# Fused attention and two expert layers: the last two of five value products moved one step later

## The chip, the cores and the metric

The kernel runs on one NeuronCore of a Trainium2 chip. The metric is device time in microseconds (us). The engines are named as in the profile: PE (TensorE, matmuls and transposes), PEld (its weight loads), DVE (VectorE), ACT (ScalarE), POOL (GpSimd), SP (SyncE, which issues the DMAs).

## The reference

Three layers in a row, in float32:

- Attention for 4 batches of 8 heads, sequence 576, head size 64: `scores = q @ k.T / 8 + decay`, causally masked, softmax over the keys, times `v`. The decay comes from a running sum of log forget gates.
- A soft mixture of experts over the 2304 tokens of width 512: `logits = x @ phi` for 32 slots, a softmax over the *tokens* (dispatch) that makes 32 slot inputs, 8 small experts, and a softmax over the slots (combine).
- A second mixture: 4 dense experts 512 to 1024 to 512, weighted by given probabilities.

## The kernel before, in words

**Pairs and steps.** Attention works on pairs of heads, `pr` from 0 to 15, four pairs to a batch. A pair has seven steps (`NS`), `g = 7 * pr + st`. A step computes the scores of one head's block of queries: step 0 the first two blocks of 128 queries of the even head, step 1 the fourth, step 2 the third, step 3 the last 64 queries of both heads together (`j == 4`), steps 4 to 6 the odd head's blocks in the order of steps 0 to 2. The main loop (L490) does, for every `g`: `scores(g)`, then `before_tr(g)`, then `transposes(g - 2)`, then `after_tr(g)`. So the transposes in step `st` belong to the scores of two steps before, and what `before_tr` and `after_tr` do belongs to the pair before.

**One step's chain.** `scores` runs two products of reduced-precision parts on PE into one of four PSUM tiles (L227, L228; L212 for step 3). DVE adds the mask and takes the maximum (L198, in two pieces for step 3), ACT computes the exponential with its row sums (L202). Two steps later PE transposes the probabilities (L249 for the first two blocks, L253 for the others, L260 for the last 64 columns) into one of two PSUM tiles; DVE or ACT copies them to SBUF, to `pta` (two blocks) or `ptb` (the other three).

**Values.** `av_a` (L289, step 1 of the next pair) multiplies the first two blocks by `v`; `av_b` (L277, step 2) does the other three blocks, 320 query columns, as five products over the five blocks of keys: 320 columns for the first three, 192 for the fourth, 64 columns of 64 keys for the fifth, each for two heads, each as two PE instructions. They add up in one PSUM tile. After the fifth ACT copies the sum into `ot` (L280) and SP loads `v` of the next pair into the one buffer there is for it (L133). `av_a` of the next pair is its first reader.

**After the values.** `nat` transposes `ot` back and DVE scales it by the row sums into `xn`, the rows of `x` (L304, L310). `logits` multiplies `ot` by `phi` (L325), and for a batch's last pair `rep4` lays the logits out for transposes. In the first pair of the next batch the finished batch's dispatch softmax runs: `dlog` transposes the logits (step 2, L372) and has DVE and ACT take maximum and exponential (L376, L381), `csoft1` and `csoft2` do the combine softmax, `dnat` transposes the exponentials back (step 4, L396, copied at L398), and `sadd` adds the tokens' share to the 32 slot sums (L407, L413). `xn` has one buffer, so the sums of a batch must have read it before `nat` of the next batch's first pair writes it.

**What sets the order.** In attention PE's instructions run in the order of the code (`tc.manual_schedule(engines={E.PE})`). For DVE, ACT, POOL and SP a planner of the framework orders the instructions by its own cost model and by when their inputs come; each engine then runs its list in order. The PSUM tiles of values, sums, `nat` and logits come in turn from one pool of two buffers (tag "av"), those of the transposes from another of two (tag "pt"), from which `dlog` takes one too. The splitting of the next pair's `q` and `k` into two parts each (`split_a`, `split_b`: ACT, DVE, POOL) is written between `scores` and `before_tr`, at steps 3, 4, 6 and 0, with the loads of `k` behind it; expert weights are loaded every third step until 33 tiles are there.

The functions that the change touches and their callers:

Of the kernel before, what the change touches and what calls it, by code (L numbers as in the profile page):

```python
# [18 lines left out]
NP = H // 2  # L19
# [15 lines left out]
def soft_moe_kernel(tc, a, out):  # L35
# [12 lines left out]
    with ExitStack() as top:  # L48
# [220 lines left out]
        def av_b(pr, i):  # L269
            if i == 0:  # L270
                av[pr] = tlq.tile([128, 512], F32, tag="av", name=f"avb_{pr}")
            t = av[pr]
            q0 = (0, 0, 0, 128, 256)[i]
            kk = 64 if i == 4 else 128
            b0 = 960 if i == 4 else 320 * i + q0
            for hh in range(2):
                pe.matmul(t[64 * hh:64 * hh + 64, q0:320], lhsT=v_raw[pr][:kk, i, 64 * hh:64 * hh + 64],  # L277
                          rhs=ptb[2 * pr + hh][:kk, b0:b0 + 320 - q0], start=i == 0, stop=i == 4)
            if i == 4:
                copy(EV[7], ot[pr][:, 256:576], t[:, 0:320])  # L280
                if pr + 1 < B * NP:
                    load_v(pr + 1)

        def av_a(pr, i):
            if i == 0:
                av[pr] = tlq.tile([128, 512], F32, tag="av", name=f"ava_{pr}")
            t = av[pr]
            for hh in range(2):
                pe.matmul(t[64 * hh:64 * hh + 64, 128 * i:256], lhsT=v_raw[pr][:, i, 64 * hh:64 * hh + 64],  # L289
                          rhs=pta[2 * pr + hh][:, 256 * i:256 + 128 * i], start=i == 0, stop=i == 1)  # L290
            if i < 1:
                return
            ot[pr] = ot_t
            copy(EV[0], ot[pr][:, 0:256], t[:, 0:256])
            ri = sm.tile([128, 5, 2], F32, tag="ri", bufs=2, name=f"ri_{pr}")
            h0 = 2 * pr % 6
            dve.tensor_scalar(ri, rs[:, :, h0:h0 + 2], 1e-9, None, op0=ALU.add)
            dve.reciprocal(ri, ri)
            rinv[pr] = ri

        def nat_pe(pr):
            t = tlq.tile([128, 4, 128], F32, tag="av", name=f"nat_{pr}")
            for c in range(4):
                pe.transpose(t[:, c, :], ot[pr][:, START[c]:START[c] + 128], ident)  # L304
            return t

        def nat_dve(pr, t):
            b, p = divmod(pr, NP)
            r = rinv[pr][:, 0:4, :, None].to_broadcast([128, 4, 2, 64])
            dve.tensor_tensor(  # L310
                xn[b][:, 0:4, 128 * p:128 * p + 128].rearrange("p c (h d) -> p c h d", d=64),
                t.rearrange("p c (h d) -> p c h d", d=64), r, op=ALU.mult)

        def nat(pr):
            b, p = divmod(pr, NP)
            if p == 0:
                xn[b] = xnp.tile([128, 5, DM], F32, tag="xn", name=f"xn_{b}")
            nat_dve(pr, nat_pe(pr))

        def plog(pr):  # L320
            b, p = divmod(pr, NP)
            t = tlq.tile([128, 512], F32, tag="av", name=f"pl_{pr}")
            pe.transpose(t[:, 384:512], ot[pr][:, 512:640], ident)
            for c in range(5):
                pe.matmul(t[:, 64 * c:64 * c + 64], lhsT=ot[pr][:, START[c]:START[c] + 128], rhs=phi2[:, p, :])  # L325
            pln = wk.tile([128, 5, 2, 32], F32, tag="pln", bufs=1, name=f"pln_{pr}")
            dve.tensor_tensor(pln, t[:, 0:320].rearrange("p (c h s) -> p c h s", c=5, h=2),
                              rinv[pr][:, :, :, None].to_broadcast([128, 5, 2, 32]), op=ALU.mult)
            if p == 0:
                lg = wk.tile([128, 5, 32], F32, tag="lg", name=f"lg_{b}")  # L330
                lb[b] = dict(lg=lg)
            lg = lb[b]["lg"]
            if p == 0:
                pool.tensor_tensor(lg, pln[:, :, 0], pln[:, :, 1], op=ALU.add)
            else:
                pool.tensor_tensor(lg, lg, pln[:, :, 0], op=ALU.add)
                pool.tensor_tensor(lg, lg, pln[:, :, 1], op=ALU.add)
            dve.tensor_tensor(xn[b][:64, 4, 128 * p:128 * p + 128].rearrange("p (h d) -> p h d", d=64),
                              t[:64, 384:512].rearrange("p (h d) -> p h d", d=64),
                              rinv[pr][:64, 4, :, None].to_broadcast([64, 2, 64]), op=ALU.mult)  # L340

        def rep4(b):
            l4 = wk.tile([128, 5, 4, 32], F32, tag="dt", name=f"l4_{b}")
            pool.tensor_scalar(l4, lb[b]["lg"][:, :, None, :].to_broadcast([128, 5, 4, 32]), 1.0, 1.0, op0=ALU.mult,
                               op1=ALU.mult)
            lb[b]["l4"] = l4

        def csoft1(b):
            lg = lb[b]["lg"]
            cm = sm.tile([128, 5], F32, tag="cm", bufs=1, name=f"cm_{b}")  # L350
            dve.tensor_reduce(cm, lg, axis=AX.X, op=ALU.max)
            ce = wk.tile([128, 5, 32], F32, tag="ce", bufs=1, name=f"ce_{b}")
            (pool if b == B - 1 else dve).tensor_tensor(ce, lg, cm[:, :, None].to_broadcast([128, 5, 32]), op=ALU.subtract)
            lb[b]["ce"] = ce
            if b < B - 1:
                act.activation(ce, ce, AF.Exp)
# [35 lines left out]
        def dnat(b):  # L392
            dt = lb[b]["dt"]
            t = tlq.tile([128, 512], F32, tag="av", name=f"dn_{b}")
            for c in range(5):
                pe.transpose(t[:ROWS[c], 32 * c:32 * c + 32], dt[0:32, START[c]:START[c] + ROWS[c]], ident[:32, :32])  # L396
            dn = wk.tile([128, 5, 32], F32, tag="pln", name=f"dnn_{b}")
            dve.tensor_copy(dn[:, 0:4, :], t[:, 0:128].rearrange("p (c s) -> p c s", c=4))  # L398
            dve.tensor_copy(dn[:64, 4, :], t[:64, 128:160])
            lb[b]["dn"] = dn  # L400

        def sadd(b, between=None):
            dn = lb[b]["dn"]
            t = tlq.tile([128, 512], F32, tag="av", name=f"sa_{b}")
            for c in range(4):
                o = 32 * c
                pe.matmul(t[o:o + 32, :], lhsT=dn[:, c, :], rhs=xn[b][:, c, :], start=True, stop=False)  # L407
            if between:
                between()
            for c in range(4):  # L410
                o = 32 * c
                n = slice(128 * c, 128 * c + 128)
                pe.matmul(t[o:o + 32, n], lhsT=dn[:64, 4, :], rhs=xn[b][:64, 4, n], start=False, stop=True)  # L413
            if b == B - 1:
                return t
            dve.scalar_tensor_tensor(s_sb, s_sb, lb[b]["al"], t, op0=ALU.mult, op1=ALU.add)

        LASTP = B * NP - 1

        def logits(pr):  # L420
            b, p = divmod(pr, NP)
            plog(pr)
            if p == NP - 1:
                rep4(b)

        def before_tr(g):

            pr, st = divmod(g, NS)
            pr -= 1
            if pr < 0:  # L430
                return
            b, p = divmod(pr, NP)
            if st == 1:
                for i in range(2):
                    av_a(pr, i)
            elif st == 2:
                for i in range(5):
                    av_b(pr, i)
            elif st == 5 and b and p == 0:
                sadd(b - 1)  # L440
            elif st == 6 and pr < LASTP:
                logits(pr)

        def after_tr(g):
            pr, st = divmod(g, NS)
            pr -= 1
            if pr >= 0 and st == 5 and pr < LASTP:
                nat(pr)
            b = pr // NP - 1
            if pr > 0 and pr % NP == 0:  # L450
                if st == 2:
                    dlog(b)
                elif st == 3:
                    csoft1(b)
                elif st == 4:
                    dnat(b)
                    dsum(b)
                    csoft2(b)
# [31 lines left out]
        for g in range(NG + 4):  # L490
            pr, st = divmod(g, NS)
# [32 lines left out]
            if LAG <= g < NG + LAG:  # L524
                transposes(g - LAG)
            after_tr(g - LAG + 2)
        order.close()
        avs.close()
# [13 lines left out]
        pr = B * NP - 1  # L542
        with tc.manual_schedule(engines={E.PE, E.Activation, E.DVE}):
            p = NP - 1
# [48 lines left out]
            i4t, st, dg, one = scr[0:32, 0:128], scr[0:32, 128:130], scr[0:32, 130:162], scr[0:32, 162:290]  # L593
# [489 lines left out]
        with tc.manual_schedule(engines={E.PE, E.Activation, E.DVE, E.Pool}):  # L1083
            for m in range(NM):
# [82 lines left out]
                if e == E2 - 1:  # L1167
                    for tt in range(2):
                        i = 2 * nb + tt
# [59 lines left out]
```

## Time and profile before

| what | value |
|---|---|
| median of 3 runs | 694.86 us (692.28 to 696.17) |
| profiled execution | 696.05 us |
| its span, first to last instruction | 694.2 us |
| mean granted TensorE clock | 0.988 of full speed |
| busy: PE, DVE, POOL, ACT | 96%, 72%, 59%, 50% of the span |

Busy time is counted over the whole span. A wait is idle time of an engine, put down to the event that ended it. The granted clock is the share of PE's full speed that the chip allowed in a stretch. In the timeline "x8" means that eight like instructions are shown as one entry, and a time in square brackets is the idle time before the entry with what ended it.

### The profile page before, as it was taken

What the parts mean: (1) busy time and instruction counts of PE and PEld (TensorE: products, weight loads), DVE (VectorE), ACT (ScalarE), POOL (GpSimd) and SP (SyncE); (2) the same over time, 40 slices, a digit from 0 to 9 for tenths busy, and PEclk for the clock granted to TensorE, in tenths of its full rate; (3) what the DMA queues carried; (4) which work ended last, traced back from release to release, by engine and by line L of the source; (5) the groups of instructions that cost most, each with busy time, mean ns of one, the idle gap of its engine ahead of it and who ended that gap; (6) DMA issues with size and microseconds to landing.
All of it is one profiled execution on the core that took longest, in us unless ns stands there. A gap on an engine that the chain in (4) does not pass through costs nothing.

```text
span 694.2 us, 15154 instructions
## 1 busy us (share of the span) xinstructions
PE 669.1 (96%) x5578; PEld 591.2 (85%) x5578; DVE 501.9 (72%) x1370; ACT 344.8 (50%) x817; POOL 412.4 (59%) x377
## 2 busy tenths in 40 slices
PE   6999999899999999999999999999999999999997
PEld 4777677677767644899999999999999999999997
DVE  7878887987878300776777976777976777977764
ACT  5766666666656102553536542446543446534441
POOL 6656565756644005972489952589843589935352
PEclk7999999999999999999999999999999999999999
DMA  6577667653325699030300030200021200001111
GB/s 199 180 232 251 200 201 228 220 172 100 97 72 197 224 417 369 1 122 1 122 3 1 7 117 9 114 2 2 20 102 29 94 2 1 32 31 61 46 48 60
DMA packets 27137, 76.14 MB, mean 110 GB/s; under 512 B 3772, under 2 KB 4156, under 8 KB 27064
## 3 DMA queue, kind: packets, MB, share of 16 engines
q1 hardware_dynamic: 27064, 75.18, 31.6%
q8 instruction: 44, 0.72, 0.4%
q14 instruction: 29, 0.24, 0.1%
HBM read 70.31 MB, written 4.72 MB: 108 GB/s over the span
## 4 chain that ended last, share of the span: by engine, by line
PE 89%; DVE 5%; issue 3%; ACT 2%; DMA 0%; POOL 0%; ACTq 0%; DVEq 0%
PE R L1019 27%; PE Q L1019 13%; PE P L1019 7%; PE avb L277 6%; PE pt L253 5%; PE two L832 5%; PE d L1039 3%; PE sc L212 3%; PE pl L325 2%; PE sc L228 2%; PE two L728 2%; PE sc L227 2%; PE pt L249 2%; PE ava L289 2%; PE so_ps L752 2%
## 5 line engine op out<-in xcount | busy, mean ns | idle before, releaser
L898 POOL TENSOR_TENSOR s<-S,s 128x512 fp32r<-128x512 f32 x136 | 174.4, 1316 | 139.5 <-ACT s L894 139.5
L894 ACT CAST s<-S 128x512 fp32r<-128x512 f32 x136 | 75.0, 619 | 87.4 <-DVE S L890 79.6
L202 ACT ACTIVATE p<-p,nm 128x256 f32<-128x256 f32 (+2 forms) x144 | 83.8, 583 | 34.4 <-DVE nm L198 33.5
L1019 PE MATMUL R<-wh_T,s 128*128 128x256 f32 x544 | 87.2, 282 | 0.5 <-DVE acc L1002 0.4
L1002 DVE SCALAR_TENSOR_TENSOR acc<-R,dpn,acc 128x256 f32<-128x256 f32 x115 | 55.4, 482 | 38.9 <-PE R L1019 36.9
L1019 PEld LDWEIGHTS R<-wh_T,s 128*128 128x128 f32 x544 | 74.3, 190 | 1.1 <-ACT a L873 1.0
L864 ACT ACTIVATE a<-two 128x256 f32<-128x256 f32 x68 | 26.1, 384 | 98.8 <-PE two L832 98.3
L198 DVE CUSTOM_DVE_ANT_0 p<-sc,maskb 128x256 f32<-128x256 f32 (+2 forms) x144 | 67.9, 486 | 3.1 <-PE sc L212 0.8
L890 DVE SCALAR_TENSOR_TENSOR S<-two,S 128x256 f32<-128x256 f32 x136 | 57.0, 419 | 3.0
L253 PE MATMUL pt<-ident,p 128*128 128x128 f32 x288 | 48.9, 289 | 9.5 <-ACT p L202 7.1
L180 POOL TENSOR_SCALAR opd<-raw 64x576 fp32r<-64x576 f32 x30 | 21.5, 715 | 61.3 <-PE sc L212 43.8
L890 DVE SCALAR_TENSOR_TENSOR S<-two,a 128x256 f32<-128x256 f32 x136 | 56.2, 413 | 0.0
L179 POOL TENSOR_TENSOR opd<-raw,opd 64x576 fp32r<-64x576 f32 x30 | 44.1, 1470 | 10.9 <-ACT opd L168 9.6
L227 PE MATMUL sc<-opd 128*128 128x256 f32 (+3 forms) x128 | 47.4, 380 | 2.4 <-ACT opd L168 2.4
L253 PEld LDWEIGHTS pt<-ident,p 128*128 128x128 f32 x288 | 31.4, 144 | 19.0 <-ACT p L202 15.2
L880 DVE SCALAR_TENSOR_TENSOR q<-two,q 128x512 fp32r<-128x512 f32 x68 | 46.2, 680 | 0.0
L832 PE MATMUL two<-c4t,gs 128*128 128x256 f32 x288 | 45.8, 281 | 0.3 <-ACT gs L168 0.3
L190 POOL TENSOR_TENSOR opd<-raw,opd 64x576 fp32r<-64x576 f32 x31 | 44.1, 1421 | 3.1 <-DVE opd L170 1.8
L1019 PE MATMUL R<-wh_T,q 128*128 128x256 f32 x272 | 44.2, 285 | 0.9 <-DVE acc L1002 0.9
L277 PE MATMUL avb<-ptb,v 128*64 128x320 f32 (+2 forms) x320 | 44.5, 378 | 0.0
L1019 PE MATMUL Q<-wh_B,s 128*128 128x256 f32 x272 | 43.6, 282 | 0.0
L1019 PE MATMUL R<-wh_B,a 128*128 128x256 f32 x272 | 43.5, 282 | 0.0
(245 smaller groups left out, 1702.4 us busy)
## 6 DMA issues: line engine op xcount, KB each, us to landing
w<-in_w SPq DMA_DIRECT2D x50, 512.0 KB
ring<-in_m SPq DMA_DIRECT2D x28, 512.0 KB
raw<-in_k SPq DMA_DIRECT2D x64, 144.0 KB
v<-in_v SPq DMA_DIRECT2D x16, 320.0 KB
out<-acc SPq DMA_DIRECT2D x18, 256.0 KB
raw<-in_q SPq DMA_DIRECT2D x15, 288.0 KB
ring<-in_w SPq DMA_DIRECT2D x8, 512.0 KB
w_opd<-in_w SPq DMA_DIRECT2D x4, 512.0 KB
```

What stands on the lines that cost most here:

```text
L198: dve.tensor_tensor_reduce(out=pt_in[j][:, k0:k0 + n], in0=sc, in1=maskb[:, m0:m0 + n], scale=-SCALE, scalar=nm, op0=ALU.add, op1=ALU.min, ...
L202: act.activation(p, p, AF.Exp, bias=nm, scale=-1.0, accum_out=sums)
L227: pe.matmul(o, lhsT=qa[hh][:, qs], rhs=ka[hh][:, 0:n], start=True, stop=False)
L253: pe.transpose(t[:, i, :], pt_in[j][:, 128 * i:128 * i + 128], ident)
L277: pe.matmul(t[64 * hh:64 * hh + 64, q0:320], lhsT=v_raw[pr][:kk, i, 64 * hh:64 * hh + 64], rhs=ptb[2 * pr + hh][:kk, b0:b0 + 320 - q0], st ...
L832: pe.matmul(t[:, j, k], lhsT=gs[e][:, 128 * fc:128 * fc + 128], rhs=c4t[:, nb * BLK:nb * BLK + BLK])
L880: dve.scalar_tensor_tensor(o[:, 1], i, 0.0, f32(o[:, 0]), op0=ALU.max, op1=ALU.subtract)
L890: dve.scalar_tensor_tensor(sv[m, name][:, c], half[m, h][:, :, k, 128 * t:128 * t + 128], 0.0, other, op0=ALU.max, op1=op)
L894: act.copy(tile_of(m, name)[:, 0], sv[m, name])
L898: (eng or pool).tensor_tensor(o[:, 1], sv[m, name], f32(o[:, 0]), op=ALU.subtract)
L1002: dve.scalar_tensor_tensor(o, t, pcol, o, op0=ALU.mult, op1=ALU.add)
L1019: pe.matmul(t, lhsT=a[:, c, :], rhs=w[:, c, :], start=first and x == 0 and c == 0, stop=x == 2 and c == 3, skip_group_check=True)
```

## The change

In the pairs' second step `av_b` runs only the products 0 to 2; products 3 and 4, with the copy into `ot` and the load of the next `v` that hang on the last, run in the third step, between the scores of step 3 and the transposes there. In the first pair of a batch (but the first batch) the slot sums `sadd` move from step 5 to step 6, still ahead of the transposes; `nat` of that pair follows them there, where it was behind step 5's transposes; and its `logits` move from step 6 to step 0 of the next pair, behind the transposes. For the other pairs `nat` and `logits` stay.

```diff
             if st == 1:
                 for i in range(2):
                     av_a(pr, i)
-            elif st == 2:
-                for i in range(5):
+            elif st in (2, 3):
+                for i in range(3) if st == 2 else range(3, 5):
                     av_b(pr, i)
-            elif st == 5 and b and p == 0:
+            elif st == 6 and b and p == 0:
                 sadd(b - 1)
+                nat(pr)
             elif st == 6 and pr < LASTP:
                 logits(pr)
 
         def after_tr(g):
             pr, st = divmod(g, NS)
             pr -= 1
-            if pr >= 0 and st == 5 and pr < LASTP:
+            b = pr // NP - 1
+            if st == 5 and 0 <= pr < LASTP and not (pr and pr % NP == 0):
                 nat(pr)
-            b = pr // NP - 1
+            if st == 0 and pr > 1 and (pr - 1) % NP == 0:
+                logits(pr - 1)
             if pr > 0 and pr % NP == 0:
                 if st == 2:
                     dlog(b)
```

## Rows read from the trace of the kernel before

**Rows 1.** The page: busy time, share of the span and instructions of each engine.

```profile
PE 669.1 (96%) x5578; PEld 591.2 (85%) x5578; DVE 501.9 (72%) x1370; ACT 344.8 (50%) x817; POOL 412.4 (59%) x377
```

**Rows 2.** Waits of PE: us in total, times, longest us.

```profile
PE pt L253 <- ACT p L202: 7.1, 11, 0.7
...
PE pt L253 <- ACT dt L381: 2.2, 3, 0.7
...
PE sa L407 <- DVE dnn L398: 1.4, 3, 0.5
```

**Rows 3.** Busy us by stretch: length, PE, PEld, DVE, ACT, POOL, granted clock, DMA share, GB/s.

```profile
72.29:89.98 17.69, 16.51 (x120) 11.67 (x119) 14.52 (x53) 10.13 (x31) 9.65 (x11) 0.90 0.64 202
...
127.78:143.90 16.12, 14.94 (x119) 10.94 (x118) 14.45 (x53) 10.05 (x31) 9.65 (x11) 1.00 0.71 237
...
156.51:169.12 12.61, 11.97 (x94) 9.60 (x93) 10.32 (x38) 8.56 (x24) 8.19 (x9) 1.00 0.34 99
...
240.00:275.00 35.00, 33.40 (x423) 14.74 (x414) 2.38 (x10) 5.12 (x13) 10.50 (x29) 1.00 1.02 414
```

**Rows 4.** Timeline of the first boundary: start us, us, engine, line, shapes, count [idle before].

```profile
79.64 0.68 ACT L381 ACTIVATE dt<-lt,dm 128x512 f32<-128x512 f32 x1
...
80.32 0.29 ACT L381 ACTIVATE dt<-lt,dm 128x64 f32<-128x64 f32 x1
...
80.76 0.55 PE L253 MATMUL pt<-ident,p 128*128 128x128 f32 x3 [0.72 <-ACT dt L381]
...
82.50 0.28 DVE L398 COPY dnn<-dn 128x128 f32<-128x128 f32 x1
...
82.83 1.72 PE L407 MATMUL sa<-xn,dnn 128*32 128x512 f32 x8 [0.46 <-DVE dnn L398]
```

**Rows 5.** Busy time by stretch, inside the first boundary.

```profile
84.00:85.00 1.00, 1.00 (x12) 0.20 (x8) 0.38 (x4) 0.81 (x2) 0.00 (x0) 0.50 0.75 184
```

**Rows 6.** Timeline of a plain pair, all engines.

```profile
61.42 2.76 PE L277 MATMUL avb<-ptb,v 128*64 128x320 f32 x20
...
64.11 0.55 PE L249 MATMUL pt<-ident,p 128*128 128x128 f32 x3
...
64.31 0.43 ACT L168 COPY ot<-avb 128x320 f32<-128x320 f32 x1 [0.87 <-PE avb L277]
...
64.41 1.34 PE L212 MATMUL sc<-opd 128*128 128x384 f32 x8
...
64.69 0.56 DVE L170 COPY pta<-pt 128x384 f32<-128x384 f32 x1 [2.00 <-PE pt L249]
...
65.88 0.83 DVE L170 CAST opd<-raw 128x576 fp32r<-128x576 f32 x1
...
66.63 0.40 DVE L198 CUSTOM_DVE_ANT_0 p<-sc,maskb,nm 128x192 f32<-128x192 f32 x1
...
67.13 0.78 ACT L202 ACTIVATE p<-p,nm 128x576 f32<-128x576 f32 x1 [0.83 <-DVE nm L198]
...
68.05 0.66 PE L253 MATMUL pt<-ident,p 128*128 128x128 f32 x4 [0.64 <-ACT p L202]
```

**Rows 7.** Instructions of L277 from 61.4 to 63.1 us, by shape.

```profile
L277 PE MATMUL avb<-ptb,v x12: 326/432/483, 61.4 to 63.1; 128*64 128x320 f32 x11, 128*64 128x192 f32 x1
```

**Rows 8.** Chain of waits, in order of time: start us, us, engine, tile, line.

```profile
58.08 0.33 PE pt L249 x3
...
64.18 0.48 PE pt L249 x3
```

**Rows 9.** Waits of PE's weight loads.

```profile
PEld avb L277 <- issue: 7.4, 29, 0.3
```

**Rows 10.** Timeline of SP and DVE: the first load, and k in a plain pair.

```profile
0.73 0.60 SPq L136 DMA_DIRECT2D fr<-in_f  x1
...
3.51 0.45 DVE L472 TENSOR_SCALAR fr<-fr 64x576 f32<-64x576 f32 x1 [3.51 <-DMA fr<-in_f]
...
163.56 3.23 SPq L128 DMA_DIRECT2D raw<-in_k  x2
```

## The prediction

> **What bounds the kernel now.** The page's busy table comes first: PE is busy for 96% of the span [rows 1], so only what PE waits for, or does at a low clock, can shorten this kernel, and the list of waits filtered to PE says where. Three of its rows lie in attention's steady part: the transposes L253 wait for the exponential L202 for 7.1 us in 11 waits, and for the exponential L381 for 2.2 us in 3; the slot sums L407 wait for a copy, L398, for 1.4 us in 3 [rows 2]. No row of that list is for the products L277.
>
> Busy time by stretch comes next, cut from one start of the products L289 to the next. A plain pair takes 12.61 us with PE busy for 11.97; the 0.64 us between is one wait. A pair that begins a new batch (three of them, called boundaries here) takes 16.12 us, PE busy for 14.94, or 17.69 us, PE busy for 16.51 at a mean granted clock of 0.90. The first boundary is shown, the third reads the same [rows 3]. The second holds the work of the other two, so a fall of the clock costs 17.69 - 16.12 = 1.57 us. In it the clock stands at half, 1.2 of 2.4 GHz, a moment after PE's two waits of that boundary, 0.72 and 0.46 us [rows 4, 5].
>
> The timeline of a plain pair shows where the 0.64 us is made [rows 6]. The five products run as one block of 2.76 us from 61.42. Behind it stand the next transposes (64.11) and the scores of step 3 (64.41). DVE meanwhile idles 2.00 us, then works off a row: copy at 64.69, a cast at 65.88, the second maximum of step 3 at 66.63. ACT starts that exponential at 67.13, and the transposes that need it start at 68.05, 0.64 us late. So PE's block starves DVE, and PE pays two steps later.
>
> **The change part by part.** The sum is made against the profiled execution, 696.05 us: a span of 694.2 and 1.85 around it. The median is 694.86, 1.2 lower; one fall of the clock less would make such a difference, which the times alone can't show.
>
> *The last two products behind step 3's scores.* Twelve instructions of 320 columns are the first three products. Up to 63.1 us eleven of them show and the first of the fourth product's, of 192 columns [rows 7], so products four and five take from 63.1 to 64.11 = 1.0 us. That much earlier come the transposes at 64.11, DVE's copy and the scores; the two products then fill 1.0 us behind the scores, and PE reaches every later instruction when it does now. The second maximum moves from 66.63 to about 65.6 and ends at 66.0; the exponential can start at 66.2, ends at 67.0, and its transposes could start at 67.1. PE is free for them at 68.05 - 0.64 = 67.4. The wait goes with 0.3 us to spare: 11 waits, 7.1 us. What is late next? DVE is busy for 10.32 of 12.61 us [rows 3], starts its run 1.0 us earlier and has to finish only 0.6 us earlier, so I see nothing.
>
> *One more change of operand shape.* The block is entered and left twice now, in 15 pairs (the last pair's two halves have nothing between them). Leaving: three transposes take 0.48 us of the chain behind the products and 0.33 behind other work [rows 8], so 0.15. Entering: weight loads of L277 show gaps put down to "issue", 7.4 us in 29, some 0.25 each [rows 9]; the matmuls hide most of it, since PE's own list has no wait for L277, so I take 0.10, nearer to the zero end. Cost: 15 x 0.25 = 3.75 us, bounds 0 and 15 x 0.40 = 6.0.
>
> *The copy of the last products (ACT) and the load of v (SP)* go a step later with them. The copy, 0.43 us, now follows the scores' cast and ends by about 66.2, just when the exponential can start; its reader, step 5's transposes, comes over 1 us later: nothing, unless the queues' order differs (rivals).
>
> *Boundary, the log terms.* Its transposes stay in step 2, so they start 1.0 us earlier, and so do the exponentials that now begin at 79.64 and 80.32; the transposes of step 4 wait for the second by 0.72 us [rows 4]. 1.0 us covers that: 2.2 us over three.
>
> *Slot sums one step later.* Their copy L398 starts at 82.50 and they start at 82.83, 0.46 us late [rows 4]. Step 5's transposes and step 6's scores now stand ahead of them, over 1 us of PE work: 1.4 us over three. Transposes (nat) and logits move behind them in the same relative order, so the PSUM tiles come round in the old order; the logits' sums are next read a pair later, and that pair covers them. Bound from the other side: DVE is busy for 14.45 us of a boundary [rows 3] that would take 15.2. If DVE becomes its limit, up to 3.6 us stay.
>
> *The clock.* With both waits gone PE works through the stretch as in plain pairs, which read 1.00 [rows 3]. I take both falls as gone: 2 x 1.57 = 3.1; the bounds are three falls (-1.6) and none.
>
> Behind attention nothing shifts against the matmuls: weights there are loaded as PE releases tiles, at 414 GB/s with PE busy for 33.40 of 35.00 us [rows 3], so the stage starts and ends earlier as one.
>
> Sum: 7.1 + 2.2 + 1.4 + 3.1 - 3.75 = 10.1 us; 696.05 - 10.1 = 686.0 us, 1.3% under the median.
>
> **A rule against it.** ACT's row at 64.31 shows a copy started when the products ended, after 0.87 us of idling [rows 6]. The Trainium skill, page "TensorE: Matmul & The Clock Gate", Part 1, architectural detail, says that ScalarE and VectorE run their queues strictly in order. By that rule whatever stands behind this copy waits for the last product too; the trace agrees as far as nothing on ACT ran in those 0.87 us. The sum above is unchanged by the rule if the copy stands behind the cast; the rival below is what it makes of the other order.
>
> **Rivals.**
> *ACT's order takes the gain back.* Today ACT runs copy, cast, exponential. Kept so, the copy would wait for the fifth product (65.6 plus about 0.2), end at 66.2, the cast at 66.9, the exponential at 67.7, its transposes start near 67.9 where now it is 68.05. The 7.1 us stay and the new shape change is paid: 693.1; part of it would give 689 to 693. For it: that is the order now. Against: in the code the scores of step 3 and their cast now come ahead of the copy. 13%.
>
> *The clock falls all the same.* Each fall is 1.57 us, and PE's work there remains thin: slot sums, transposes and logits follow each other. Two falls give 689.1, three 690.7. Against: one boundary kept its full clock with both waits in it. 14%.
>
> *Slower: v comes too late.* v is single, its load is issued when the last product is done, and the next pair's L289 needs it. SP issues in order, and the two halves of a k load hold it from 163.56 to 166.79 in a pair that ends at 169.12 [rows 3, 10]. If the v load falls behind the second half, it is issued at 166.15 (0.64 for the faster pair). The shortest load that shows from issue to use is f's, from 0.73 to 3.51 = 2.8 us [rows 10]: v at 168.95, while L289 wants it at 168.5, 0.5 us late; where a weight load of 512 KB is ahead of it, 1.25 us at 414 GB/s more, 1.7. Over 15 pairs that is 7 to 26 us, 693 to 712, say 702. It decides from the point where v lands behind the end of the pair. Against: left in its place, v is issued near 65.8 and has 5.8 us. 8%.
>
> *The change doesn't do what it says*, because the other engines' orders shift so that the second maximum stays late: the same 693, counted with the first rival.
>
> **How the numbers follow.** Forecast 60%, with its own range 682 (no cost of the shape change) to 688.5 (0.40 for each); more gain than that 5%; clock 14%; ACT's order 13%; v 8%. A measurement tells 0.5%, 3.5 us, from no change, so faster is below 691.4 and slower above 698.3. Faster: 60 + 5 + 14 and 3 of the 13 = 82%; same: the other 10; slower: 8. The range reaches from 681.5 to 691.5, past the clock's cases; beyond it lie most of ACT's order and v, and a little of the greater gain.
>
> **What would show it.** PE's wait for L202 at L253 falls from 7.1 us to under 1; a plain pair takes 12.2 us; DVE's wait of 2.00 us halves. A boundary takes about 15.2 us at clock 1.00, without waits for L381 and L398. L277 stands in two blocks, of about 1.7 and 1.0 us. Wrong: a plain pair at 12.6 or more with the exponential behind L168 (first rival), PE waiting for v at L289 (third), or a granted clock under 1.00 at the boundaries (second).

## The result, and the profile after

The change takes 688.35 us (median of 6 runs, 687.24 to 688.93), the kernel before 695.04 (6 runs): ratio 0.9911, 95% interval 0.9889 to 0.9932. That is inside the range and 2.35 us above the 686.0 forecast. The profiled execution takes 688.55 us, its span 686.8 at a mean granted clock of 0.992; before it was 694.2 at 0.988. So the profile has 7.4 us less span where 10.1 were forecast, and the rest of this document asks where the difference went.

The page after, busy time, share of the span and instructions of each engine, answers to [rows 1]:

```profile
PE 670.1 (98%) x5578; PEld 588.1 (86%) x5578; DVE 502.8 (73%) x1370; ACT 343.7 (50%) x817; POOL 412.4 (60%) x377
```

PE does as much as before (670.1 us against 669.1) in a shorter span: on balance, what went was waiting. (The busy time that two falls of the clock had cost before is gone too, but the pairs take about as much more.) PE's waits after (us in total, times, longest) answer to [rows 2]:

```profile
PE pl L323 <- DVE s_sb L416: 2.1, 3, 0.7
...
PE sa L407 <- DVE dnn L399: 0.5, 3, 0.2
```

The 7.1 and 2.2 us of the transposes L253 behind the two exponentials are gone, and of the slot sums' 1.4 us there is 0.5 left. A new wait stands above it: the logits' first matmul L323 waits 0.69 us in each of the three boundaries for the slot sums' update on DVE, L416.

Busy time by stretch after (length, PE, PEld, DVE, ACT, POOL, granted clock, DMA share, GB/s), a plain pair and the three boundaries, from one start of L289 to the next, answers to [rows 3]:

```profile
72.33:88.69 16.36, 15.50 (x120) 10.68 (x119) 15.02 (x55) 10.34 (x32) 9.56 (x10) 1.00 0.74 227
112.84:124.91 12.07, 12.07 (x93) 9.44 (x92) 10.40 (x38) 8.54 (x24) 8.19 (x9) 1.00 0.81 272
124.91:141.27 16.36, 15.51 (x120) 10.71 (x119) 15.02 (x55) 10.33 (x32) 9.53 (x10) 1.00 0.69 217
177.49:193.85 16.36, 15.50 (x120) 10.70 (x119) 15.02 (x55) 10.34 (x32) 9.54 (x10) 1.00 0.35 95
```

The plain pair has no idle PE left: 12.07 us long, 12.07 busy. The boundaries all have the full clock. But at 16.36 us each is 0.24 longer than the one boundary of before that kept its clock (16.12). Apart from the clock, the boundaries lost time.

Cut at the starts of L289, the 7.4 us of span add up so (after less before):

| part of the span | before | after | difference |
|---|---|---|---|
| up to the first L289 | 21.86 | 23.81 | +1.95 |
| 11 plain pairs | 138.66 | 133.03 | -5.63 |
| 3 boundaries | 51.50 | 49.08 | -2.42 |
| the last pair | 11.29 | 11.27 | -0.02 |
| the rest, to the end | 470.89 | 469.61 | -1.28 |

The first row is scatter: the change's own second profile (below) starts its first L289 at 21.52, and in the twelve profiles with an edit the start lies between 21.49 and 23.81.

The timeline of a plain pair after (start us, us, engine, line, shapes, count, [idle before]) answers to [rows 6]:

```profile
114.59 2.17 PE L277 MATMUL avb<-ptb,v 128*64 128x320 f32 x12
...
116.68 0.55 PE L249 MATMUL pt<-ident,p 128*128 128x128 f32 x3
...
116.99 1.31 PE L212 MATMUL sc<-opd 128*128 128x384 f32 x8
117.27 0.56 DVE L170 COPY pta<-pt 128x384 f32<-128x384 f32 x1 [1.07 <-PE pt L249]
...
118.18 0.67 ACT L168 CAST opd<-raw 64x576 fp32r<-64x576 f32 x1 [1.24 <-PE sc L212]
...
118.23 0.81 PE L277 MATMUL avb<-ptb,v 128*64 128x192 f32 x8
...
118.97 0.66 PE L253 MATMUL pt<-ident,p 128*128 128x128 f32 x4
...
119.19 0.40 DVE L198 CUSTOM_DVE_ANT_0 p<-sc,maskb,nm 128x192 f32<-128x192 f32 x1
119.22 0.35 SPq L133 DMA_DIRECT2D v<-in_v  x1
...
119.69 0.78 ACT L202 ACTIVATE p<-p,nm 128x576 f32<-128x576 f32 x1 [0.83 <-DVE nm L198]
...
120.46 0.41 ACT L168 COPY ot<-avb 128x320 f32<-128x320 f32 x1
...
120.70 0.60 PE L253 MATMUL pt<-ident,p 128*128 128x128 f32 x4
```

DVE's idle time before the copy fell from 2.00 to 1.07 us. The transposes behind the exponential start at 120.70 with nothing to wait for. On ACT the order is cast (118.18), exponential (119.69), copy of the last products (120.46).

### The profile page after: what moved, and what is told of

It reads as the page before. It is cut to its first block, busy times and chain, and to the rows that moved or that the text cites. A ratio compares the mean times of both kernels' runs of the same rounds, so it can differ in the third digit from the quotient of the medians.

```text
span 686.8 us, 15142 instructions
## 1 busy us (share of the span) xinstructions
PE 670.1 (98%) x5578; PEld 588.1 (86%) x5578; DVE 502.8 (73%) x1370; ACT 343.7 (50%) x817; POOL 412.4 (60%) x377
## 4 chain that ended last, share of the span: by engine, by line
PE 89%; DVE 7%; issue 2%; SPq 1%; ACT 1%; DMA 0%; POOL 0%; ACTq 0%; DVEq 0%
PE R L1022 27%; PE Q L1022 13%; PE P L1022 7%; PE avb L277 6%; PE pt L253 5%; PE two L835 5%; PE d L1042 3%; PE sc L228 3%; PE sc L212 3%; PE sc L227 2%; PE pl L325 2%; PE two L731 2%; PE ava L289 2%; PE so_ps L755 2%; PE pt L249 2%
## 5 line engine op out<-in xcount | busy, mean ns | idle before, releaser
L179 POOL TENSOR_TENSOR opd<-raw,opd 64x576 fp32r<-64x576 f32 x30 | 44.5, 1483 | 17.7 <-ACT opd L168 16.4
L190 POOL TENSOR_TENSOR opd<-raw,opd 64x576 fp32r<-64x576 f32 x31 | 44.0, 1420 | 10.0 <-DVE opd L170 8.7
L253 PE MATMUL pt<-ident,p 128*128 128x128 f32 x288 | 48.8, 289 | 0.5 <-DVE ptb L170 0.5
L277 PE MATMUL avb<-ptb,v 128*64 128x320 f32 (+2 forms) x320 | 47.8, 383 | 0.0
L180 POOL TENSOR_SCALAR opd<-raw 64x576 fp32r<-64x576 f32 x30 | 20.5, 685 | 40.4 <-PE sc L212 30.2
L1022 PE MATMUL R<-wl_T,s 128*128 128x256 f32 x272 | 43.5, 282 | 0.0
```

The lines of the kernel that those rows point to most:

```text
L253: pe.transpose(t[:, i, :], pt_in[j][:, 128 * i:128 * i + 128], ident)
L1022: pe.matmul(t, lhsT=a[:, c, :], rhs=w[:, c, :], start=first and x == 0 and c == 0, stop=x == 2 and c == 3, skip_group_check=True)
```

## What the new boundary shows

The timeline of the second boundary after, the instructions on the way to the wait of L323:

```profile
131.43 0.31 DVE L351 TENSOR_REDUCE cm<-lg 128x5 f32<-128x160 f32 x1
...
131.95 1.50 POOL L179 TENSOR_TENSOR opd<-raw,opd 64x576 fp32r<-64x576 f32 x1
...
132.44 1.20 DVE L353 TENSOR_TENSOR ce<-lg,cm 128x160 f32<-128x160 f32 x1
...
136.67 0.16 DVE L362 TENSOR_SCALAR cs<-cs 128x5 f32<-128x5 f32 x1
...
137.11 1.42 POOL L179 TENSOR_TENSOR opd<-raw,opd 64x576 fp32r<-64x576 f32 x1 [0.98 <-ACT opd L168]
...
137.62 1.09 DVE L364 TENSOR_TENSOR cn<-ce,cs 128x160 f32<-128x160 f32 x1
...
138.63 0.73 DVE L416 SCALAR_TENSOR_TENSOR s_sb<-s_sb,al,sa 128x512 f32<-128x512 f32 x1
...
139.42 0.33 PE L323 MATMUL pl<-ident,ot 128*128 128x128 f32 x1 [0.69 <-DVE s_sb L416]
```

L416 reads the slot sums' PSUM tile; that pool has two tiles, and the logits, two allocations later, need this one. Ahead of L416 on DVE stands the second part of the combine softmax (csoft2: L361 to L364). Its last product L364 takes 1.09 us here. Before, the same instruction took 0.32 with POOL idle, and the add L362, which takes 0.16 here, took 0.80 beside POOL. The timeline of the first boundary before:

```profile
79.91 1.49 POOL L179 TENSOR_TENSOR opd<-raw,opd 64x576 fp32r<-64x576 f32 x1
...
80.62 0.80 DVE L362 TENSOR_SCALAR cs<-cs 128x5 f32<-128x5 f32 x1
...
84.06 0.32 DVE L364 TENSOR_TENSOR cn<-ce,cs 128x160 f32<-128x160 f32 x1
```

In each case the long one starts inside a POOL instruction and ends with it or just behind: L362 at 81.42 where POOL ends at 81.40, L364 at 138.71 where POOL ends at 138.53, L353 at 133.64 where POOL ends at 133.45. So part of DVE's busy time here is time in which it is held: 0.77 of the 1.09 us of L364, by its 0.32 before. Two theories can be told apart by runs: DVE's row ahead of L416 makes the wait, by its order and by this holding; or the two PSUM tiles come round too late whatever DVE does. A third is the bound of the prediction, that DVE has too much work per boundary (15.02 us of 16.36).

## The experiments

**The two halves alone.** First only the split of the products, on the kernel before:

```diff
-            elif st == 2:
-                for i in range(5):
+            elif st in (2, 3):
+                for i in range(3) if st == 2 else range(3, 5):
```

> The kernel before with the products split alone; sums, nat and logits of a batch stay in their old steps. Theory (the block of products starved DVE): plain pairs fall from 12.61 to 12.07 us, as in the change, with no wait of PE for the exponential of step 3. At the boundaries the wait of 0.72 us for the log terms' exponential goes, the 0.46 us for the copy L398 stays or grows. If one of the two waits was enough to drop the clock, it still falls at one or two boundaries (17.5 us each); if it takes both, it stays at 1.00 (about 16.1). Time 687.5 to 690. Rival (the plain pairs gain from the new order of the queues that the moved sums bring): plain pairs stay at 12.6 and the time above 692.

689.09 us (5 rounds), ratio 0.9897, 0.9869 to 0.9925: by itself as good as the whole change. PE's waits and busy time by stretch:

```profile
PE sa L407 <- DVE dnn L399: 3.4, 3, 1.1
...
PE ava L289 <- DMA v<-in_v: 0.8, 2, 0.6
```

```profile
72.39:88.56 16.17, 15.05 (x119) 10.72 (x118) 14.53 (x55) 10.13 (x31) 10.02 (x11) 1.00 0.74 239
...
124.81:142.59 17.78, 16.66 (x119) 11.61 (x118) 14.60 (x55) 10.14 (x31) 10.03 (x11) 0.90 0.66 216
```

The plain pairs take 12.06 to 12.10 us, but for one of 12.77 that waits for v. In the boundary the wait for L381 is gone, the slot sums wait 1.12 us instead of 0.46, and one of three clocks fell.

Then the change without the split (the same lines the other way round):

> The change without the split: all five products in step 2, the sums, nat and logits of a batch moved. Theory: plain pairs stay at 12.61 us with PE's wait of 0.64. At the boundaries the wait for the log terms (0.72 us) stays, the wait for L398 goes, the combine softmax's first part keeps its place in DVE's idle time before the copy of the first two blocks, so no new wait for L416 stands before the logits; boundary 15.6 to 16.0 us at clock 1.00. Time 690.5 to 693. Rival (two PSUM tiles in turn, not DVE's queue, make the new wait before the logits): that wait, 0.69 us, is there too, boundary 16.3 or more, time 692 to 695.

692.7 us (10 runs), ratio 0.9961, 0.9939 to 0.9983. PE's waits and busy time by stretch:

```profile
PE pt L253 <- ACT p L202: 7.2, 11, 0.7
PE pt L253 <- ACT dt L381: 2.2, 3, 0.7
```

```profile
72.73:88.37 15.64, 14.92 (x120) 10.93 (x119) 14.26 (x54) 10.50 (x33) 9.21 (x11) 1.00 0.68 213
...
234.00:237.00 3.00, 2.94 (x27) 1.73 (x30) 0.29 (x1) 0.00 (x0) 0.57 (x2) 0.53 0.49 127
```

Alone, the boundary half works as planned: the slot sums' wait is gone, a boundary takes 15.64 us at full clock, and L323 does not wait. The clock fell instead at the start of the first expert layer. So neither half makes the wait of L323; it comes from both together. With the split, L351 and L353 leave DVE's idle time ahead of the copy into pta (131.06 for L353 before) and stand in the dense row around the second maximum. In the whole change L364 then starts at 137.62, beside POOL's L179 and ahead of L416; with the split alone L416 stands ahead of L364, and with the shift alone L364 (0.32 us) is done 0.72 us before L416 starts.

**Four and one products instead of three and two** (`range(4)`, `range(4, 5)`).

> The change with four products in step 2 and only the fifth moved. Theory: the fifth takes 0.3 to 0.5 us of PE, so DVE's idle time before the copy of the first two blocks falls from 2.00 to 1.5 to 1.7 us (1.07 with three and two), and PE's wait for step 3's exponential shrinks by as much, to 0.1 to 0.35 us: plain pairs 12.2 to 12.4 us. Rival (what counts is the new order of the other engines' queues, not how early the scores come): plain pairs 12.07 as in the change, or 12.6 as before.

688.29 us (one run). The plain pair is 12.34 us as expected, with part of the old wait back; DVE's idle time before the copy is 1.75 us, a little over the 1.5 to 1.7 expected. PE's waits and a plain pair by stretch:

```profile
PE pt L253 <- ACT p L202: 2.0, 8, 0.3
```

```profile
59.72:72.06 12.34, 12.10 (x93) 9.64 (x92) 10.31 (x38) 8.45 (x24) 8.19 (x9) 1.00 0.70 227
```

The time is that of the change all the same, for the boundaries take 15.72 us each where the change has 16.36. The timeline of the first one shows the main difference:

```profile
84.91 0.31 DVE L364 TENSOR_TENSOR cn<-ce,cs 128x160 f32<-128x160 f32 x1
...
85.94 0.33 PE L323 MATMUL pl<-ident,ot 128*128 128x128 f32 x1
```

L364 stands ahead of L416 here as after the change, but POOL is idle from 83.42 to 86.27. It takes 0.31 us, and L323 waits 0.14 us at most. So L364 in that place costs little when nothing runs beside it.

**The combine softmax's second part behind the logits**, in step 0 of the next pair:

```diff
             if st == 0 and pr > 1 and (pr - 1) % NP == 0:
                 logits(pr - 1)
+                csoft2((pr - 1) // NP - 1)
...
-                    csoft2(b)
```

> The change, with the second part of the combine softmax (L361 to L364) moved from step 4 of the boundary to behind the logits in step 0 of the next pair. Theory (DVE's queue makes the new wait): L364, 1.09 us, no longer stands ahead of L416, PE's wait of 0.69 us before the logits falls under 0.2 us and the boundary from 16.36 to 15.6 to 15.9 us; the next pair, where DVE has idle time, stays at 12.1. Rival (the two PSUM tiles in turn make it): the wait stays near 0.69 us and the boundary at 16.3.

> The kernel with the combine softmax's second part behind the logits, timed. Theory: boundaries stay at 15.45 us, three times 0.9 below the change, plain pairs 12.08: 2 to 3.5 us below the change run beside it, 684 to 686.5. Rival (its single time of 684.57 came from an early start of attention and no fall of the clock): within 1 us of the change.

684.57 us in the single run; 686.4 in five rounds, ratio 0.9865, 0.9833 to 0.9897, an interval that overlaps the change's. L323 does not wait and the boundary takes 15.45 us (15.6 to 15.9 was expected), so the PSUM tiles are not it. One boundary of six, in the second profile, takes 15.98 us: there the exponential L381 came late, and PE waited 0.79 us for it; why is not shown. A boundary by stretch:

```profile
69.81:85.26 15.45, 15.28 (x120) 10.70 (x119) 14.11 (x53) 10.59 (x34) 10.87 (x11) 1.00 0.69 217
```

**One instruction moved.** To tell DVE's own work from its holding, only L364 was put there; every other instruction of DVE keeps its order. The edit, shortened:

```diff
-            dve.tensor_tensor(cn[:, b], ce, cs..., op=ALU.mult)        # csoft2, L364
+        def csoft3(b): dve.tensor_tensor(cn[:, b], ce, cs..., op=ALU.mult)
...
                 logits(pr - 1)
+                csoft3((pr - 1) // NP - 1)
```

> The change with one instruction moved on DVE: the last product of the combine softmax (L364) stands behind the logits' copies instead of ahead of the slot sums' update (L416). After the change L364 takes 1.09 us there, beside POOL's L179, against 0.32 us with POOL idle. Theory (L364 is held for 0.77 us while POOL's two-input instruction runs, and that is what makes L416 late): the whole 0.69 us wait of the logits L323 goes, the boundary falls from 16.36 to 15.4 to 15.7 us, the time of this run to about 686 to 687. Rival (it is DVE's own work ahead of L416 that counts, 0.32 us of L364 in it): 0.37 us of the wait stays, boundary about 16.0 us. Rival (PSUM tiles come round too late whatever DVE does): wait and boundary as after the change, 0.69 and 16.36 us. Plain pairs 12.08 us in all three.

The boundaries take 15.45, 15.44 and 15.44 us and the wait is gone: 0.91 us each for an instruction that takes 0.32 by itself (0.69 of it is the wait, and PE is busy for 0.21 us less, 15.29). Its timeline and busy time by stretch:

```profile
82.53 1.42 POOL L179 TENSOR_TENSOR opd<-raw,opd 64x576 fp32r<-64x576 f32 x1 [0.98 <-ACT opd L168]
...
83.03 0.74 DVE L416 SCALAR_TENSOR_TENSOR s_sb<-s_sb,al,sa 128x512 f32<-128x512 f32 x1
...
83.98 0.27 PE L323 MATMUL pl<-ident,ot 128*128 128x128 f32 x1
...
85.84 1.40 POOL L190 TENSOR_TENSOR opd<-raw,opd 64x576 fp32r<-64x576 f32 x1 [1.89 <-DVE opd L170]
...
86.87 1.03 DVE L364 TENSOR_TENSOR cn<-ce,cs 128x160 f32<-128x160 f32 x1
...
87.20 0.52 POOL L334 TENSOR_TENSOR lg<-pln 128x160 f32<-128x160 f32 x1
```

```profile
70.32:85.77 15.45, 15.29 (x120) 10.73 (x119) 14.11 (x55) 10.44 (x33) 9.55 (x10) 1.00 0.73 230
```

L416 starts inside POOL's L179, as L364 did, and takes its usual 0.74 us. L364 takes 1.03 in its new place, again beside POOL: it starts during L190, POOL goes on with L334 without a pause, and L364 ends 0.18 us behind L334. Nobody waits for it there. The run's time, 688.12, missed the 686 to 687 expected: the clock fell at the start of the first expert layer (L731 from the ring: median 518 ns, after the change 379), and from the last L289 on this run takes 4.2 us more than the change.

**The first part earlier.** `csoft1(b - 1)` is called in step 1 of the boundary instead of step 3, so L353 runs before the copy into pta and L364 stands one maximum earlier.

> The change with the combine softmax's first part (L351, L353) put in step 1 of the boundary instead of step 3; its second part moves up by one score of step 5 with it, so that L364 stands one maximum earlier on DVE, in the same boundary. DVE has as many instructions per boundary as after the change. Theory (order and holding, not amount of work, make L416 late): L364 starts ahead of POOL's L179 and takes about 0.32 us, the 0.69 us wait of L323 goes, the boundary takes 15.2 to 15.7 us. Rival (DVE has become the limit of the boundary by the amount of its work, 15.0 us of 16.4): a wait of PE on DVE stays, boundary 16.0 to 16.4 us. Plain pairs 12.08 us in both.

> The change with the combine softmax's first part in step 1 of the boundary, timed in five rounds. Theory: boundaries 15.21 us each, 3 x 1.15 = 3.5 us under the change's, which has 688 to 689 us as median: 685 to 686 us, ratio to before 0.985 to 0.988. Rival (what the boundaries win is given back behind attention): 688 to 689 us, ratio 0.991.

685.28 us, and in five rounds 685.2 (684.71 to 685.6), ratio 0.9852, 0.9832 to 0.9871: better than the change, whose interval begins at 0.9889. Boundary by stretch, and its timeline:

```profile
71.03:86.24 15.21, 15.21 (x120) 10.82 (x119) 15.15 (x56) 10.89 (x34) 9.71 (x11) 1.00 0.72 222
```

```profile
82.21 0.31 DVE L364 TENSOR_TENSOR cn<-ce,cs 128x160 f32<-128x160 f32 x1
...
83.00 1.42 POOL L179 TENSOR_TENSOR opd<-raw,opd 64x576 fp32r<-64x576 f32 x1 [0.83 <-ACT opd L168]
...
83.25 0.73 DVE L416 SCALAR_TENSOR_TENSOR s_sb<-s_sb,al,sa 128x512 f32<-128x512 f32 x1
...
84.45 0.27 PE L323 MATMUL pl<-ident,ot 128*128 128x128 f32 x1
```

DVE is busy for 15.15 of 15.21 us, more than after the change, and PE waits for nothing. So the amount of DVE's work was not the limit; L364 starts 0.79 us ahead of POOL's L179, takes 0.31, and L416 is in time.

**Both moves together.**

> The change with the combine softmax's second part behind the logits and its first part (L351, L353) already in step 1 of the boundary, ahead of DVE's idle time. Theory (the first part left DVE's idle time of 1.07 us and made the stretch behind it denser): L353 takes 0.67 us again in place of 1.20, the wait of 0.17 us for L399 goes too, boundary 15.2 to 15.4 us, time 0.3 to 1 us under that of the second part alone. Rival (PE is the limit at 15.45 already): boundary and time as with the second part alone.

685.94 us, ratio 0.9874, 0.9837 to 0.9912; boundaries 15.21 and 15.22. Moving the second part as well adds nothing to moving the first alone. L353 did not fall to the 0.67 us expected: it takes 1.45, as it starts 0.12 us into POOL's L190, but PE waits nowhere in the boundary.

**Two and three products**, on the late second part:

> The second part of the combine softmax behind the logits, and the split after two products, three moved. Theory: PE's wait for the exponential is gone with three and two already, so more room for DVE buys nothing: DVE's idle time falls from 1.07 to 0.5 to 0.8 us, plain pairs 12.0 to 12.15 us, boundaries 15.3 to 15.6. Rival (the fewer products ahead, the better): plain pairs under 11.95 us.

A miss: 688.85 us, plain pairs of 12.48 instead of 12.0 to 12.15. The boundaries, 15.33 and 15.32, are as expected; DVE's idle time is 0.86 to 0.88 us, over the 0.5 to 0.8 expected. PE's waits:

```profile
PE pt L253 <- ACT ptb L168: 2.2, 9, 0.2
...
PE pt L253 <- DVE ptb L170: 0.6, 2, 0.3
```

The first block is now too short: the copies out of an earlier step's transposes are not done when PE comes back to L253, 0.25 to 0.31 us in each of the eleven plain pairs, nine times for ACT and twice for DVE; PE's busy time is 12.23 for 12.07. Three products cover both ends.

**The change once more.**

> The change itself, once more. If the late start of attention in its profile (first value products at 23.81 us, 21.86 before) is scatter of the start and not made by the change, it moves to between 21.5 and 23.5 here, as it did from 21.49 to 23.34 in the four experiments; if the change makes it, it is 23.5 or more again. Plain pairs 12.07 and boundaries 16.36 us as before, no fall of the clock at the boundaries. Time 686.5 to 689.

689.15 us, ratio 0.991, 0.9879 to 0.9942; boundaries 16.36, 16.34 and 16.35, the first L289 at 21.52. PE's waits:

```profile
PE pl L323 <- DVE s_sb L416: 2.1, 3, 0.7
PE ava L289 <- DMA v<-in_v: 1.2, 2, 0.6
```

The wait of L323 is the same to a hundredth; the waits for v were not in the first profile. The time is just over the 686.5 to 689 expected. Three of its six executions took 690.1 to 690.42 us, at mean granted clocks of 0.990 and 0.987, where the others have 0.992 to 0.995.

## Why the prediction was right, and where its sum was off

*The plain pair's wait, 7.1 us: right, by the mechanism named.* All eleven are gone, the DVE wait before the copy halved (1.07 for 2.00), the second maximum no longer late. The split alone brings it and the shift alone does not. The two blocks are 2.09 and 0.74 us from start to the next PE instruction, not 1.7 and 1.0. The first three products run as before (their twelfth and last instruction starts 1.74 us behind the first, before and after), but the transposes start 0.36 us behind that one; and the moved two need 0.74 where the text had read 1.0. What came earlier came 0.93 us earlier, by DVE's idle time.

*The change of operand shape, 0.25 us a pair: mis-sized.* It measured 0.10, the growth of PE's busy time in a plain pair (12.07 for 11.97; 15.05 for 14.94 in a boundary with the split alone). The forecast for the eleven was 4.3 us (11 x (0.64 - 0.25)); they gave 5.63. The forecast had 0.15 for leaving the block, from one comparison of transposes in the chain [rows 8], and 0.10 for entering it; no run tells the two apart.

*The clock, 3.1 us: as forecast in the profiles, but not shown to be the change's.* The clock fell in no boundary after the change, nor in its second profile. What the rows show beside it: two of three boundaries fell before, one of three with the split alone, where PE waited 1.12 us in one piece; none in the other nine profiles with an edit. In three of those nine the clock fell at the start of the first expert layer instead. What decides in which stretch it falls stays open. The timed executions set a bound: at one mean granted clock, 0.993, eight of the kernel before took 692.16 to 694.59 us and three of the change 687.33 to 688.93. So some 5 us of the 6.7 between the medians come without the clock, as the pairs and boundaries have it at full clock (5.63 - 0.72 = 4.9), and the clock's part is nearer 1.5 than 3.1 us, by estimate. That the profiled pair shows the whole 3.1 is in part luck.

*The boundary, 15.2 us: this step failed.* It took 16.36, 3 x 1.16 = 3.5 us over the three, and so the boundaries gave 2.42 us of the 5.95 forecast (2.2 + 1.4 + 3.1 - 0.75). The old waits went as said, all but 0.16 us of the slot sums'; the 1.16 us are the waits of 0.69 and 0.16 us and 0.31 us more of PE's busy time (15.50) than the 15.19 that the sum implies. The text set the range of this term right, "If DVE becomes its limit, up to 3.6 us stay", and took the wrong end; its reason was wrong too, for DVE has 15.15 us busy in a boundary of 15.21 without making PE wait. What it left out is what stands ahead of L416 once the split has moved csoft1, and that L364's price depends on whether POOL runs beside it. That L364 is held is what the runs tell best: moving 0.32 us of DVE's work would have given back some 0.3 us of each boundary, and moving it gave 0.91; and with four and one products, where POOL is idle beside it, it took 0.31 us in its place ahead of L416 and left L323 a wait of 0.14. With it out of the way the boundary is 15.45; with csoft1 in DVE's idle time it is 15.21, what the forecast had, by an edit that it did not have.

*Sum.* Forecast 10.1, measured 7.5 on the two profiled executions: plain pairs 1.3 better, boundaries 3.5 worse, the last pair 0.3 better (no cost where 0.25 was set down); the start cost 1.95 by scatter and the end gave 1.28, which no run ties to the change. So the time lies inside the range although the boundaries' term was wrong by 3.5 us.

*The rivals.* ACT's order did not stay as it was: it is now cast (118.18), exponential (119.69), copy (120.46). The Trainium skill's rule on strict queues (page "TensorE: Matmul & The Clock Gate", Part 1, architectural detail) had nothing to take here: with the copy behind the exponential, the transposes that need the exponential start at 120.70 without a wait. The clock did not fall in the boundaries of the two profiles. The late v exists but is small: waits of 0.17 to 0.64 us, two in the change's second profile, two with the split alone and one in one of the later runs, none in the first profile. In the change's second profile v is issued at 116.69, behind two weight loads of 512 KB issued at 114.81, and L289 waits until 123.11. That the weights slow it is read from the order, not tested.

## What to carry to other kernels

A wait that goes moves the engine that made it too: after a step is moved, list what now stands ahead of every instruction that frees a buffer, and not only what the moved step itself waits for. Busy time is no measure of an engine's limit where its instructions can be held by another engine's; look for one form whose duration comes in two sizes, and see what runs beside the long one. Where a block is cut in two, both halves have something to cover: a plain pair takes 12.07 us with three and two products, 12.34 with four and one, 12.48 with two and three.

## What the runs showed of the hardware

Beside an idle POOL, DVE's L364 takes 0.30 to 0.32 us and L362 0.15 or 0.16; beside a POOL instruction up to 1.09 and 0.81. L353, never beside an idle POOL, takes 0.58 to 1.56. In the boundaries of all thirteen profiles, wherever one of the three starts while POOL's instruction runs, it ends 0.03 us (L362) or 0.17 to 0.19 us (L353, L364) behind POOL's end, whether it started early or late in it: L353 started 0.1 us into a POOL instruction takes 1.46 us, started 0.9 us into one 0.67. With L364 behind the logits that end is L334's, which follows L190 at once. The instruction beside them is mostly one with two inputs (L179, L190); in four cases it is L180, which has one, and L353 takes 0.58 to 0.62 us.

The Trainium skill, page "SBUF — State Buffer", section "Who interferes with whom", says that a VectorE instruction with two inputs in SBUF contends with a GpSimd instruction that reads SBUF, and that the ports the two engines share are an exclusive lock. The trace agrees: L353 and L364 read two SBUF tensors and are held to the end, L416 reads one of its two from PSUM and took 0.74 us inside POOL's L179. For L362, which has one input, the same section names the instruction among those that can take a mode with the same effect where their operands allow it; its 0.80 us agrees with that.
